# Five first slices of w1 issued from two queues, and one warm-up matmul fewer, in a SiLU MLP with its gradients

## The chip, the core and the metric

The kernel runs on one core of one Trainium2 chip. The metric is the device time of one execution in microseconds, as the median of several executions. The compute engines are TensorE (PE; its weight loads are listed apart as PEld), VectorE (DVE), ScalarE (ACT) and GpSimd (POOL). SyncE (SP) here only issues DMA transfers. ScalarE can issue them too, from a queue of its own. "SPq" and "ACTq" in the profile are the issuing of transfers by these two engines.

## The reference

```python
B, S, D, F = 1, 2048, 640, 1536          # all bf16
def _fwd_reference(x, w1, w2):
    h = jnp.einsum("bsd,df->bsf", x, w1)
    h = jax.nn.silu(h)
    out = jnp.einsum("bsf,fd->bsd", h, w2)
    return out

def reference(x, w1, w2, grad_out):
    _out, _vjp = jax.vjp(_fwd_reference, x, w1, w2)
    return (_out, *_vjp(grad_out))       # out, grad x, grad w1, grad w2
```

It is a two-layer perceptron with SiLU between the layers, forward and backward.

## The kernel before

The 2048 rows are worked in four chunks `c` of 512 (`SC`). For a chunk, TensorE computes h (line 204: `w1` slices times the transposed x), ScalarE makes a = silu(h) (line 213) and, with VectorE, the factor of the derivative (lines 217 to 220). TensorE then computes the gradient of a (line 254, finished by VectorE on line 261) and, in `sd_phase` (line 270), the chunk's out and its grad x. The transposed a, grad h, out and grad x go through DRAM scratch tensors (`aT_scr`, `ghT_scr`, `oT_scr`, `gxT_scr`) and come back transposed by DMA. After the four chunks two long stages make grad w2 (line 359) and grad w1 (lines 389 and 408). A matmul here has 128 x 128 weights and, nearly always, 512 columns.

The order of the instructions on each engine is that of the program as the tile framework schedules it, and each DMA issued takes one of eight completion semaphores in turn ("lanes"). A DMA that reuses a lane waits for the transfer that had it before.

What matters here is the head of the program, lines 143 to 210:

- Before the kernel's body the engines meet at an entry wait. `start_before_entry_wait` (line 16) takes the instructions of a given list, with what stands ahead of them on the same engine, and puts them in front of that engine's entry wait. The list is called `early`.
- VectorE fills a tile `warm` (line 144). TensorE runs `NWARM` = 21 matmuls of 128 columns on it (line 148), whose results nobody reads.
- SP issues the load of the first 128 rows of x (`x_nat`, q = 0) and ScalarE that of the next 128 (q = 1), line 171.
- SP then loads the first 1024 columns (`GC`) of w1 in slices of 128 rows: slices 0, 1 and 2 by one DMA each, ahead of the entry wait, and slices 3 and 4 together by one DMA after it (lines 177 and 178). A slice is 128 x 1024 bf16, 256 KB.
- Behind them on SP follow a DMA transpose that fills the second half of the first chunk's xT (line 179), the other 512 columns of w1 (line 180), w2 (line 183), the first chunk of grad_out transposed (line 184) and the transposed weights (lines 186 and 187).
- ScalarE, after its one load, loads its table and runs a small SiLU (line 182).
- `pe_x` (line 189): TensorE transposes the two loaded blocks of x in ten matmuls (line 195) into three PSUM tiles, and VectorE, ScalarE and VectorE copy these to the first half (`HC` = 256 columns) of xT (line 200). The first copy holds the rows of D that slice 0 of w1 meets, the second those of slices 1 and 2, the third those of slices 3 and 4.
- `h_first` (line 230): for slice after slice of w1, eight matmuls (ft 0 to 7) of 256 columns on that first half (line 235). So slice k is first needed by the matmul of number 8k, counted from 0. The eight sums need all eight PSUM banks: ft 6 takes the bank that ScalarE's copy empties. After the 40 matmuls of this kind come those on the second half of xT (line 237).

Of the kernel before, what the change touches and what calls it, by code (L numbers as in the profile page):

```python
# [15 lines left out]
def start_before_entry_wait(nc, names):  # L16

    def move(nc):
        blocks = nc.m.functions[0].blocks
        entry, home = blocks[0].instructions, blocks[1].instructions
        for engine in {i.engine for i in home if i.name in names}:
            mine = [i for i in home if i.engine == engine]
            last = max(k for k, i in enumerate(mine) if i.name in names)
            moved = mine[: last + 1]
            gate = next(
                k
                for k, i in enumerate(entry)  # L30
                if i.engine == engine and isinstance(i, mybir.InstEventSemaphore)
            )
            taken = {i.name for i in moved}
            for k in reversed(range(len(home))):
                if home[k].name in taken:
                    del home[k]
            for i in reversed(moved):
                entry.insert(gate, i)

    nc.at_finalize(move)  # L40
# [22 lines left out]
def kernel(  # L63
# [11 lines left out]
    nc = tc.nc  # L75
# [8 lines left out]
    F = w1.shape[1]  # L84
    ST, DT, FT = S // P, D // P, F // P
# [4 lines left out]
    NFC = F // FC  # L90
    FB = FC // P
    LAG = 2
    NWARM = 21
    HC = 2 * P
    NG = 8
    NCOPY = FT - NG
    GC = NG * P
# [16 lines left out]
    w1_v = w1.rearrange("(dt p) f -> p dt f", p=P)  # L114
# [19 lines left out]
    with ExitStack() as mctx:  # L134
# [9 lines left out]
        early = [nc.vector.memset(warm[:], 1.0)]  # L144
        warm_a = cpool.tile([P, 1], FP32, name="warm_a")
        wp = ps_h.tile([P, SC], FP32, name="wp", tag="hp")
        for i in range(NWARM):
            early.append(nc.tensor.matmul(wp[:, 0:P], lhsT=warm[:], rhs=warm[:], start=True, stop=True))  # L148
# [4 lines left out]
        w1_nat = w1pool.tile([P, DT, F], dt_in, name="w1_nat", tag="w1a")  # L153
# [16 lines left out]
        def load_x(eng, q):  # L170
            return eng.dma_start(out=x_nat[:, q, :], in_=x_v[:, q, :])

        def load_w1(lo, hi, cols):
            return nc.sync.dma_start(out=w1_nat[:, lo:hi, cols], in_=w1_v[:, lo:hi, cols])

        early += [load_x(nc.sync, 0), load_x(nc.scalar, 1)]
        early += [load_w1(k, k + 1, slice(0, GC)) for k in range(3)]
        load_w1(3, DT, slice(0, GC))
        nc.sync.dma_start_transpose(out=xT_next[:, :, HC:SC], in_=x2[HC:SC, :])
        load_w1(0, DT, slice(GC, F))  # L180
        start_before_entry_wait(nc, {i.ins.name for i in early})
        nc.scalar.activation(warm_a[:], warm[:, 0:1], ACT.Silu)
        nc.sync.dma_start(out=w2_nat[:], in_=w2_v[:])
# [101 lines left out]
        for c in range(NCH):  # L285
# [15 lines left out]
            if c == 0:  # L301
                h_first(xT, aT, ghT)
                nc.sync.dma_start(
                    out=aT_scr[:, c * SC:(c + 1) * SC].rearrange("(ft p) s -> p ft s", p=P), in_=aT[:]
                )
                sd_phase(c, w2_nat, aT, oT_scr)
                for ft in range(FT):
                    g_group(ft, goT, ghT)
                nc.sync.dma_start(
                    out=ghT_scr[:, c * SC:(c + 1) * SC].rearrange("(ft p) s -> p ft s", p=P), in_=ghT[:]  # L310
# [4 lines left out]
            for i in range(FT + LAG):  # L315
# [7 lines left out]
                out=aT_scr[:, c * SC:(c + 1) * SC].rearrange("(ft p) s -> p ft s", p=P), in_=aT[:]  # L323
            )
            nc.sync.dma_start(
                out=ghT_scr[:, c * SC:(c + 1) * SC].rearrange("(ft p) s -> p ft s", p=P), in_=ghT[:]
# [7 lines left out]
    with ExitStack() as fctx:  # L334
# [17 lines left out]
        k = 0  # L352
# [26 lines left out]
        k = 0  # L379
        for fc in range(NFC):  # L380
            gh_blk = gh_blks[fc]
            for dt_ in range(DT):
                if dt_ == DT // 2:
                    store_gw2(fc)
                if fc == NFC - 1 and dt_ == DT - 1:
                    for k, (lo, hi) in enumerate(((0, FC - P), (FC - P, FC))):
# [12 lines left out]
                        else:  # L399
                            nc.vector.tensor_copy(out=g1[:, lo:hi], in_=gp[:, lo:hi])  # L400
                        last_store = nc.sync.dma_start(
                            out=gw1_v[:, dt_, fc * FC + lo:fc * FC + hi], in_=g1[:, lo:hi]
# [49 lines left out]
```

## Time and profile before

| What | Value |
|---|---|
| median of 5 runs | 320.8 us (320.39, 320.17, 320.8, 321.26, 320.91) |
| the profiled execution | 320.42 us, of which the profile's span is 318.6 us |
| TensorE busy | 314.0 us of the span |
| VectorE, ScalarE, GpSimd busy | 103.1, 77.2 and 0.7 us |
| DMA | 67.02 MB, mean 210 GB/s |

Times within the profile are counted from the start of its span, in microseconds. A timeline merges instructions of one kind that follow each other: it gives the start, the time from the first start to the last end, the engine, the line, the operation, what it writes and reads, and the count. In brackets stands the idle time before it and what ended that. The time of a DMA issue is that of the issuing engine; the transfer itself lands later, which the list of DMA issues tells as microseconds from issue to landing.

### The profile page before, as it was taken

What the parts mean: (1) busy time and instruction counts of PE and PEld (TensorE: products, weight loads), DVE (VectorE), ACT (ScalarE), POOL (GpSimd) and SP (SyncE); (2) the same over time, 40 slices, a digit from 0 to 9 for tenths busy, and PEclk for the clock granted to TensorE, in tenths of its full rate; (3) what the DMA queues carried; (4) which work ended last, traced back from release to release, by engine and by line L of the source; (5) the groups of instructions that cost most, each with busy time, mean ns of one, the idle gap of its engine ahead of it and who ended that gap; (6) DMA issues with size and microseconds to landing.
All of it is one profiled execution on the core that took longest, in us unless ns stands there. A gap on an engine that the chain in (4) does not pass through costs nothing.

```text
span 318.6 us, 3597 instructions
## 1 busy us (share of the span) xinstructions
PE 314.0 (99%) x1499; PEld 149.3 (47%) x1527; DVE 103.1 (32%) x182; ACT 77.2 (24%) x139; POOL 0.7 (0%) x6
## 2 busy tenths in 40 slices
PE   9999999999999999999999999999999999999996
PEld 8744444444444444444444444444444444444443
DVE  1594641477410187700147741000000100001001
ACT  2781000644201354311064420111100001001100
POOL 0000000000000000000000000000000000000000
PEclk9999999999999999999999999999999999999999
DMA  9989999999899866382534089919999999997211
GB/s 245 347 170 213 236 264 246 347 288 309 249 238 320 211 207 165 105 290 84 165 115 134 0 273 263 208 30 294 248 240 255 241 216 347 220 264 218 67 39 45
DMA packets 147729, 67.02 MB, mean 210 GB/s; under 512 B 113921, under 2 KB 147073, under 8 KB 147713
## 3 DMA queue, kind: packets, MB, share of 16 engines
q1 hardware_dynamic: 147568, 66.62, 82.6%
q8 instruction: 12, 0.20, 0.2%
q10 hardware_dynamic: 144, 0.16, 0.1%
q14 instruction: 5, 0.03, 0.0%
HBM read 9.18 MB, written 28.97 MB: 120 GB/s over the span
## 4 chain that ended last, share of the span: by engine, by line
PE 99%; issue 1%; DVE 0%; DVEq 0%
PE hp L270 32%; PE hp L204 16%; PE hp L254 16%; PE hp L359 16%; PE hp L408 15%; PE hp L389 1%; PE wp L148 1%; PE tp L195 0%; DVE g L400 0%; DVE warm L144 0%; DVEq L400 0%; DVEq L436 0%
## 5 line engine op out<-in xcount | busy, mean ns | idle before, releaser
L204 PE MATMUL hp<-xT,w_nat 128*128 128x512 bf16 (+1 forms) x272 | 57.5, 352 | 0.4
L254 PE MATMUL hp<-goT,w2T 128*128 128x512 bf16 x238 | 56.8, 379 | 0.1
L270 PE MATMUL hp<-aT,w_nat 128*128 128x512 bf16 x235 | 52.2, 379 | 0.3
L270 PE MATMUL hp<-ghT,w1T 128*128 128x512 bf16 x236 | 52.2, 379 | 0.2
L359 PE MATMUL hp<-a_blk,go_nat 128*128 128x512 bf16 x235 | 51.7, 379 | 0.3
L408 PE MATMUL hp<-gh_blk,x_nat 128*128 128x512 bf16 x220 | 48.3, 379 | 0.2
L278 ACT ACTIVATE oT<-hp 128x512 bf16<-128x512 f32 x24 | 14.3, 598 | 106.5 <-PE hp L270 106.5
L204 PEld LDWEIGHTS <-w_nat 128*128 128x128 bf16 x280 | 27.8, 100 | 25.0 <-DMA w_nat<-in_w_dram 0.2
L213 ACT ACTIVATE aT<-hp 128x512 bf16<-128x512 f32 x48 | 28.6, 606 | 36.0 <-PE hp L204 36.0
L270 PEld LDWEIGHTS <-w1T 128*128 128x128 bf16 x240 | 23.5, 98 | 28.3
L254 PEld LDWEIGHTS <-w2T 128*128 128x128 bf16 x240 | 23.5, 98 | 28.3
L359 PEld LDWEIGHTS <-go_nat 128*128 128x128 bf16 x240 | 23.5, 98 | 28.3
L270 PEld LDWEIGHTS <-w_nat 128*128 128x128 bf16 x240 | 23.4, 98 | 28.4
L261 DVE SCALAR_TENSOR_TENSOR ghT<-ghT,hp 128x512 bf16<-128x512 bf16 x48 | 32.5, 682 | 7.3 <-PE hp L254 7.3
L280 DVE CAST oT<-hp 128x512 bf16<-128x512 f32 x16 | 11.1, 692 | 72.4 <-PE hp L270 72.4
L408 PEld LDWEIGHTS <-x_nat 128*128 128x128 bf16 x224 | 21.9, 98 | 26.4
L220 DVE SCALAR_TENSOR_TENSOR ghT<-aT,v 128x512 bf16<-128x512 bf16 x48 | 32.6, 687 | 0.3
L219 DVE TENSOR_SCALAR v<-t 128x512 bf16<-128x512 f32 x48 | 20.2, 426 | 27.7 <-ACT t L217 27.7
L217 ACT ACTIVATE t<-hp 128x512 f32<-128x512 f32 x44 | 26.1, 598 | 0.5 <-DVE v L219 0.5
L419 DVE CAST g<-hp 128x512 bf16<-128x512 f32 x7 | 4.8, 692 | 47.0 <-PE hp L408 26.6
L369 DVE CAST g2T<-hp 128x512 bf16<-128x512 f32 x7 | 4.8, 692 | 46.1 <-PE hp L359 46.1
L367 ACT ACTIVATE g2T<-hp 128x512 bf16<-128x512 f32 x8 | 4.8, 597 | 47.0 <-PE hp L359 47.0
(22 smaller groups left out, 27.1 us busy)
## 6 DMA issues: line engine op xcount, KB each, us to landing
aT_scr<-aT SPq DMA_DIRECT2D x4, 1536.0 KB, 6.3
ghT_scr<-ghT SPq DMA_DIRECT2D x4, 1536.0 KB, 8.1
out_dram<-o_sb SPq DMA_DIRECT2D x8, 640.0 KB, 3.4
oT_scr<-oT SPq DMA_DIRECT2D x4, 640.0 KB, 4.3
go_nat<-in_grad_out_dram SPq DMA_DIRECT2D x4, 640.0 KB, 6.5
gxT_scr<-oT SPq DMA_DIRECT2D x4, 640.0 KB, 5.0
w_nat<-in_w_dram SPq DMA_DIRECT2D x1, 1920.0 KB, 12.8
x_nat<-in_x_dram SPq DMA_DIRECT2D x3, 640.0 KB, 7.2
```

Of the source, the lines that this page charges most:

```text
L204: nc.tensor.matmul(hp[:, cols], lhsT=w1_nat[:, dt_, ft * P:(ft + 1) * P], rhs=xT[:, dt_, cols], start=(dt_ == 0), stop=(dt_ == DT - 1),)
L213: nc.scalar.activation(aT[:, ft, :], hp[:], ACT.Silu)
L217: nc.scalar.activation(t[:], hp[:], ACT.Tanh, scale=0.5)
L219: nc.vector.tensor_scalar(out=v[:], in0=t[:], scalar1=-0.5, scalar2=0.5, op0=ALU.mult, op1=ALU.add)
L220: nc.vector.scalar_tensor_tensor(out=ghT[:, ft, :], in0=aT[:, ft, :], scalar=1.0, in1=v[:], op0=ALU.subtract, op1=ALU.mult)
L254: nc.tensor.matmul(gp[:], lhsT=w2T[:, dt_, ft * P:(ft + 1) * P], rhs=goT[:, dt_, :], start=(dt_ == 0), stop=(dt_ == DT - 1),)
L261: nc.vector.scalar_tensor_tensor(out=ghT[:, ft, :], in0=ghT[:, ft, :], scalar=1.0, in1=gp[:], op0=ALU.add, op1=ALU.mult)
L270: nc.tensor.matmul(op_[:], lhsT=w_all[:, ft, dt_ * P:(dt_ + 1) * P], rhs=rhs_all[:, ft, :], start=(ft == 0), stop=(ft == FT - 1),)
L278: nc.scalar.activation(oT[:, dt_, :], op_[:], ACT.Copy)
L280: nc.vector.tensor_copy(out=oT[:, dt_, :], in_=op_[:])
L359: nc.tensor.matmul(gp[:], lhsT=go_nat[:, st, dt_ * P:(dt_ + 1) * P], rhs=a_blk[:, st, :], start=(st == 0), stop=(st == ST - 1),)
L408: nc.tensor.matmul(gp[:], lhsT=x_nat[:, st, dt_ * P:(dt_ + 1) * P], rhs=gh_blk[:, st, :], start=(st == 0), stop=(st == ST - 1),)
```

## The change

The five slices of w1 become five DMAs. Slices 0, 2 and 3 are issued by SP and slices 1 and 4 by ScalarE, all ahead of the entry waits. One warm-up matmul is dropped.

```diff
-    NWARM = 21
+    NWARM = 20
...
-        def load_w1(lo, hi, cols):
-            return nc.sync.dma_start(out=w1_nat[:, lo:hi, cols], in_=w1_v[:, lo:hi, cols])
+        def load_w1(eng, lo, hi, cols):
+            return eng.dma_start(out=w1_nat[:, lo:hi, cols], in_=w1_v[:, lo:hi, cols])
 
         early += [load_x(nc.sync, 0), load_x(nc.scalar, 1)]
-        early += [load_w1(k, k + 1, slice(0, GC)) for k in range(3)]
-        load_w1(3, DT, slice(0, GC))
+        for k, eng in enumerate((nc.sync, nc.scalar, nc.sync, nc.sync, nc.scalar)):
+            early.append(load_w1(eng, k, k + 1, slice(0, GC)))
         nc.sync.dma_start_transpose(out=xT_next[:, :, HC:SC], in_=x2[HC:SC, :])
-        load_w1(0, DT, slice(GC, F))
+        load_w1(nc.sync, 0, DT, slice(GC, F))
         start_before_entry_wait(nc, {i.ins.name for i in early})
```

In the built program SP has one instruction fewer and ScalarE has two DMA issues more, ahead of its entry wait and its table load. SP still has four DMAs ahead of its own entry wait. The lanes of all later transfers move on by one, and so do their waits. In two places SP's order changes: the transpose of x for chunk 2 (line 160) stands ahead of the store of chunk 0's out (line 281) instead of behind it, and the transpose of grad_out for chunk 2 (line 165) ahead of the store of chunk 0's grad h (line 309).

## The prediction

> **What bounds the kernel now.** I read the page first (span, busy times, chain), then the timeline of the first 22 us, then the head again by weight loads, by half-microsecond windows and by DMA issues.
>
> ```profile
> span 318.6 us, 3597 instructions
> ...
> PE 314.0 (99%) x1499; PEld 149.3 (47%) x1527; DVE 103.1 (32%) x182; ACT 77.2 (24%) x139; POOL 0.7 (0%) x6
> ...
> PE 99%; issue 1%; DVE 0%; DVEq 0%
> ```
>
> TensorE is the bound from end to end. All that a change of the loads can touch is TensorE's idle or slow time in the head, so the head is read instruction by instruction (timeline; start, length, engine, line, count):
>
> ```profile
> 0.09 0.40 SPq L171 DMA_DIRECT2D x_nat<-in_x_dram  x1
> 0.21 0.38 ACTq L171 DMA_DIRECT2D x_nat<-in_x_dram  x1
> ...
> 0.50 2.42 PE L148 MATMUL wp<-warm 128*128 128x128 bf16 x21 [0.50 <-DVE warm L144]
> 0.54 1.89 SPq L174 DMA_DIRECT2D w_nat<-in_w_dram  x4
> ...
> 0.74 1.28 ACT L182 ACT_TABLE_LOAD   x1 [0.74 <-DVEq L436]
> ...
> 2.47 1.49 SPq L179 DMA_TRANSPOSE xT<-in_x_dram  x1
> ...
> 2.72 1.27 PE L195 MATMUL tp<-ident,x_nat 128*128 128x128 bf16 x10
> 3.60 0.85 DVE L200 COPY xT<-tp 128x256 bf16<-128x256 bf16 x2 [3.16 <-PE tp L195]
> ...
> 3.81 0.59 ACT L200 COPY xT<-tp 128x512 bf16<-128x512 bf16 x1 [1.58 <-PE tp L195]
> ...
> 7.51 10.11 PEld L204 LDWEIGHTS <-w_nat 128*128 128x128 bf16 x76 [0.20 <-DMA w_nat<-in_w_dram]
> ```
>
> TensorE starts at 0.50 and from then on waits for data in one listed place: 0.20 us before the weight load at 7.51, the first use of slice 3. That is 0.20 us of the loader. A load normally follows the last by 0.109 us here (next view), so the matmul row loses about 0.20 - 0.11 = 0.09 us. The first matmul on h starts at 3.94, just after the first copy of xT ends (a copy of 0.29 us from 3.60, so 3.89). The weight loads, one for each matmul, tell TensorE's pace:
>
> ```profile
> 4.11 1.65 PEld L204 LDWEIGHTS <-w_nat 128*128 128x128 bf16 x8
> 5.80 1.52 PEld L204 LDWEIGHTS <-w_nat 128*128 128x128 bf16 x14
> ```
>
> Eight loads from 4.11 to 5.80 are (5.80 - 4.11) / 8 = 0.211 us each; from 5.80 on it is (1.52 - 0.10) / 13 = 0.109. So TensorE runs at half pace until 5.80, though the profile's granted clock reads 1.00 in every row. A microsecond lost or won before 5.80 is worth half a microsecond of work. The DMA side, by windows (TensorE, weight loads, VectorE, ScalarE, GpSimd, clock, DMA share, GB/s) and by issues (time from issue to landing last):
>
> ```profile
> 2.00:2.50 0.50, 0.50 (x7) 0.50 (x6) 0.00 (x0) 0.22 (x2) 0.00 (x0) 1.00 1.07 373
> 2.50:3.00 0.50, 0.50 (x7) 0.47 (x6) 0.00 (x0) 0.00 (x0) 0.00 (x0) 1.00 1.06 408
> ```
>
> ```profile
> w_nat<-in_w_dram SPq DMA_DIRECT2D x3, 256.0 KB, 3.7
> ...
> w_nat<-in_w_dram SPq DMA_DIRECT2D x1, 512.0 KB, 5.4
> ...
> x_nat<-in_x_dram SPq DMA_DIRECT2D x1, 160.0 KB, 2.6
> x_nat<-in_x_dram ACTq DMA_DIRECT2D x1, 160.0 KB, 2.8
> ```
>
> ```profile
> w_nat<-in_w_dram SPq DMA_DIRECT2D x1, 256.0 KB, 3.2
> ```
>
> The last line is slice 0 alone: 0.54 + 3.2 = 3.74. The five copies of line 174 land after 3.2, 3.7, 4.6, 5.4 and 6.6 us: slice 1 at about 1.0 + 3.7 = 4.7, slice 2 at 1.47 + 4.6 = 6.1, slices 3 and 4 at 2.04 + 5.4 = 7.4. The DMA engines are full from 2.0 on. Slices 3 and 4 are late because of the bytes ahead of them, not because of when they are issued.
>
> **The change part by part.**
>
> *One warm-up matmul fewer.* Its pace is (2.72 - 0.50) / 21 = 0.106 us. The first transpose would be free to start at 2.61, but x lands at 0.09 + 2.6 = 2.69, so it gains 0.03 us of wall time, at half pace 0.015. Bounds: 0, and 0.106 / 2 = 0.05 if x lands earlier. I take 0.015, by the landing row.
>
> *Slices 3 and 4 issued ahead of the entry wait.* SP issues its fourth slice at about 1.47 instead of 2.04, ScalarE slice 4 earlier still. With the engines full (1.07, 1.06) the same 320 KB of x and 1280 KB of w1 must pass before the fifth slice is in. If the engines take the two queues in turn, the order is x, x, slice 0 (SP), 1 (ACT), 2 (SP), 4 (ACT), 3 (SP): the one that is needed first of the last two comes last. So slice 3 lands where the pair landed. Bounds: 0, and all of the 0.09 us if slice 3 comes ahead of 4. I take 0, by the two full windows.
>
> *Slice 0 now has a rival for the engines.* Slice 1, from ScalarE at about 0.65, can run beside slice 0 from SP at 0.54. The two x blocks show how two queues share: issued 0.12 apart they landed at 2.69 and 0.21 + 2.8 = 3.01, one after the other and not both at the end. That speaks for slice 0 keeping its 3.74; it may come as late as 3.89, when the xT copy ends, at no cost. Bounds: 0, and slice 1 wholly ahead, 256 KB at 373 GB/s = 0.70 us, landing 4.44: 4.44 - 3.91 = 0.53 us of wait, half of that 0.26. I take 0.
>
> The Trainium skill speaks against the change, in "DMA: Bandwidth & Descriptors", section "Issuing engines are not separate DMA queues": transfers from several engines run on the same 16 DMA engines and interleave, and several issuers save only the issuing time. By it the sum below stays; by a reading of two queues as twice the bandwidth slice 3 would be 0.09 us to the good.
>
> *What is queued behind ScalarE's two new issues.* At SP's spacing (0.54 + 1.89 for four, so 0.47 each) they delay ScalarE's table load from 0.74 to about 1.7; it ends at 3.0 and the small SiLU (0.2 us) at 3.2. The next work of ScalarE is its xT copy at 3.81, released by TensorE: 0.6 us of cover, cost 0. Were the cover gone, the copy's result is wanted only by slice 1, eight matmuls after 3.94 (about 5.6), and its bank by ft 6 at 3.94 + 6 x 0.211 = 5.2; it ends at 4.40 now. Another 0.8 us is free, then it costs half of each microsecond.
>
> *What moves on SP.* One DMA less after the entry wait: the xT transpose, the rest of w1, w2 and grad_out are issued some 0.4 us earlier, into engines that are full. The rest of w1 now waits for the lane of the second x block (3.01, before SP gets there at 3.6), w2 for the first x block's, grad_out for slice 1's (4.7, wanted at about 6.5). Cost 0.
>
> *The two swaps in the middle of SP's order.*
>
> ```profile
> 43.65 0.59 SPq L281 DMA_DIRECT2D oT_scr<-oT  x1
> 44.33 8.45 SPq L160 DMA_TRANSPOSE xT<-in_x_dram  x1
> ```
>
> The store goes behind an issue of 8.45 us, and the read-back of it, next but one on SP, waits for its landing (8.0 us in the list of the oT issues) some 5 us longer. The store's buffer is written again at 85.5 by ScalarE, over 25 us later; the grad h store slips in the same way from 63.2, by the 7.25 us of its transpose and these 5 us, and its buffer is next written in chunk 2, after 108. Cost 0.
>
> Sum against the profiled execution: 318.6 - 0.015 + 0 + 0 + 0 = 318.6 of span, and the 1.8 us that lie outside it (320.42 - 318.6) stay. That execution is 0.4 us under the median of 320.8. The forecast is thus the median itself, 320.8, with 320.8 - 0.05 - 0.09 = 320.7 and 320.8 + 0.26 = 321.1 as bounds of the known terms. The five runs spread over 1.09 us; I give the forecast 320.4 to 321.4.
>
> **The rivals.**
>
> *Slice 0 comes late and TensorE speeds up later (slower).* Place: the first load of line 204, at 3.77. The wait costs 0.26 at most by itself. But if the full pace is granted for activity, a hole before 5.80 may put it off. It came 5.80 - 0.50 = 5.3 us after the first matmul; put off by d it costs d / 2, between 0 and 2.65 us, and I take the middle, 1.3. Then 320.8 + 0.2 + 1.3 = 322.3. It decides from a landing of slice 0 after about 3.9. For it: slice 0 has only 0.15 us of slack. Against it: the order of the x blocks, and a hole that the head already has between transposes and h (ten transposes at 0.106 from 2.72 end at 3.78, so 3.94 - 3.78 = 0.16 us).
>
> The Trainium skill, "TensorE: Matmul & The Clock Gate", Part 1, holds that the full clock comes after a busy window of 3.4 us that runs free of the kernel. By it one missed window costs 3.4 / 2 = 1.7 us, an estimate, and this rival would give 322.7.
>
> *TensorE speeds up earlier (faster).* The same dependence, with x and the slices a little earlier and the waits gone. Known gains end at 0.05 + 0.09 = 0.14, too little to be told. Only an earlier pace change can do more: at best at 3.94, (5.80 - 3.94) / 2 = 0.93, so 319.9. Nothing in the head gets denser except by 0.03 us, so mostly the spread of the runs speaks for it.
>
> *The third slice's wait does go.* Slice 3 ahead of 4: 320.8 - 0.09 - 0.015 = 320.7, within no change.
>
> **How the numbers follow.** What a measurement of this kernel can tell from no change is about 0.2%, 0.64 us. Forecast with the last rival: 0.48. Late slice 0 or a later pace: 0.32, as it has the larger price. Earlier pace, or a median that falls on the low side: 0.20. The predicted time is 320.8. The range runs from 320.0, most of the way to 319.9, up to 322.0, within the slower case.
>
> **What would show it.** The wait before slice 3 near 7.4 still there and on a DMA: the shared engines are right. Slice 0 landing after 3.9 and a wait before the first load of line 204: the slower rival. The pace of the weight loads changing far from 5.8: the pace decides, in either direction. A wait of ScalarE's copy at 3.81 for its table, or any TensorE wait after 8 us, would make my cover wrong.

## The result, and the profile after

The changed kernel took 320.99 us (median of 27 runs, 320.38 to 323.62) against 320.61 us for the kernel before in the same comparison (46 runs, 320.17 to 321.26). The ratio is 1.0021 with a 95% interval of 1.0011 to 1.003: slower by about 0.2%. It agrees with the averages of the runs, 321.30 and 320.64 us; the medians differ by 0.38 us, or 0.12%. The fastest runs of the two kernels lie 0.2 us apart, but ten of the 27 runs took 321.4 us or more, and the kernel before has none there. The loss is in the upper part of the spread, so a typical run loses less than a bad one.

The profiled execution of the changed kernel is one of these: 321.77 us with a span of 320.0, so again 1.8 us lie outside. The page, in its span, busy times and chain:

```profile
span 320.0 us, 3597 instructions
...
PE 314.0 (98%) x1498; PEld 149.0 (47%) x1526; DVE 103.0 (32%) x182; ACT 77.2 (24%) x139; POOL 0.7 (0%) x6
...
PE 96%; DMA 2%; issue 1%; ACTq 0%; DVE 0%; DVEq 0%
```

TensorE is as busy as before, 314.0 us. What is new is a DMA share in the chain. The head, in the timeline (columns as before):

```profile
0.54 1.36 SPq L174 DMA_DIRECT2D w_nat<-in_w_dram  x3
0.62 0.94 ACTq L174 DMA_DIRECT2D w_nat<-in_w_dram  x2
...
1.67 1.28 ACT L182 ACT_TABLE_LOAD   x1 [1.67 <-ACTq L436]
2.04 2.19 SPq L179 DMA_TRANSPOSE xT<-in_x_dram  x1
2.83 0.98 PEld L195 LDWEIGHTS <-x_nat 128*128 128x128 bf16 x10 [0.27 <-DMA x_nat<-in_x_dram]
...
3.90 0.59 ACT L200 COPY xT<-tp 128x512 bf16<-128x512 bf16 x1 [0.73 <-PE tp L195]
...
4.41 1.40 PEld L204 LDWEIGHTS <-w_nat 128*128 128x128 bf16 x8 [0.60 <-DMA w_nat<-in_w_dram]
4.41 1.68 PE L204 MATMUL hp<-xT,w_nat 128*128 128x256 bf16 x8 [0.34 <-DMA w_nat<-in_w_dram]
...
7.11 1.97 PEld L204 LDWEIGHTS <-w_nat 128*128 128x128 bf16 x19 [1.30 <-DMA w_nat<-in_w_dram]
7.12 2.14 PE L204 MATMUL hp<-xT,w_nat 128*128 128x256 bf16 x18 [1.02 <-DMA w_nat<-in_w_dram]
```

Two waits stand where there was none: before the first load on slice 0 (at 4.41) and, after exactly eight loads, before the first load on slice 1 (at 7.11). The wait before slice 3, near 7.5 in the kernel before, is gone; slice 3 is wanted only near 8.8 now. In the kernel before, the loads of line 204 up to that wait form one row:

```profile
3.77 3.54 PEld L204 LDWEIGHTS <-w_nat 128*128 128x128 bf16 x24
```

These are all the waits of TensorE and its loader on a DMA in the changed kernel, over the whole span (engine, line, what was waited for; us in total, times, longest):

```profile
PEld L204 <- DMA w_nat<-in_w_dram: 1.9, 2, 1.3
PE hp L204 <- DMA w_nat<-in_w_dram: 1.4, 2, 1.0
PEld L195 <- DMA x_nat<-in_x_dram: 0.3, 1, 0.3
```

The last is the wait for x ahead of the transposes (x was in at 2.79, before at 2.64). It is over well before slice 0 is in.

The difference of the two spans, 320.0 - 318.6 = 1.4 us, is accounted for as follows. The pace changes from half to full at about 5.8 in both profiles. By then the kernel before has begun ten weight loads of line 204 and the changed one eight; two at 0.109 us make 0.22. The loads on slice 1 start 1.30 us after the last one ended, and the profile before loses 0.11 there by its normal spacing: 1.19. The 0.09 before slice 3 is won. Together 0.22 + 1.19 - 0.09 = 1.32 of 1.4.

Why the two slices are late is told by the issues, each in a window of its own: engine, size, us from issue to landing. The first is slice 0, the second slice 1:

```profile
w_nat<-in_w_dram SPq DMA_DIRECT2D x1, 256.0 KB, 3.8
```

```profile
w_nat<-in_w_dram ACTq DMA_DIRECT2D x1, 256.0 KB, 6.5
```

Slice 1 was issued at 0.62, earlier than before, and landed at 7.1; before, it landed at 4.7. The DMA queues between 3 and 4 us show its new path (queue: packets, MB, share of 16 engines; q1 holds what SP issues, q10 what ScalarE issues). First the kernel before, then the changed one:

```profile
q1 hardware_dynamic: 184, 0.33, 112.0%
```

```profile
q10 hardware_dynamic: 107, 0.20, 61.1%
q1 hardware_dynamic: 64, 0.10, 34.6%
```

Before, all 0.33 MB of that microsecond came through SP's queue. After, two thirds came through ScalarE's. These bytes are slice 1's, and by themselves no loss: slice 1 is the second to be needed. A slice is spread over 16 DMA engines, and TensorE goes on only when the last of them has reported: the loads start at 4.41 and 7.11, 0.04 us after the last reports of slices 0 and 1, at 4.37 and 7.07. The trace's semaphore records give that report for each engine; here are the landing times of each slice, as the median of the 16 engines, the 13th and the last (us):

```
             slice 0            slice 1            slice 2            slice 3            slice 4
before       3.53 3.59 3.73     4.18 4.36 4.74     5.12 5.95 6.08     7.43 7.45 7.47 (3 and 4 together)
changed      3.51 3.61 4.37     4.31 4.83 7.07     5.29 5.58 7.27     8.38 8.56 8.61     5.92 8.33 8.37
```

The typical engine kept nearly the old order and the old times for slices 0 to 2. Most engines worked off one transfer after the other: between 3.2 and 3.8 us the records count 77 packets of q10, slice 1's, and only 15 of q1. A few engines fell behind, and these decide. The 2 KB packets from 6.56 to 7.2 us form three chains, each with a packet every 0.08 us, and in each chain q10 and q1 alternate strictly: an engine with work left in both queues serves them by turns here.

The chain that closes slice 1 last can be followed back by the packets' times (the records don't name the engine). Slice 1's first packet started at 4.07 and took 1.47 us instead of 0.08. Its other seven started from 5.62 to 6.58, 0.16 us apart, with slice 2's eight packets between them. So the engine lost 1.39 us to one long packet and, by an estimate from these numbers, 8 x 0.08 = 0.64 us to the turns with slice 2. In one queue, slice 2 would have stood behind slice 1. By this estimate the turns are about half of the 1.19 us; the long packet is the rest. The transpose of x, which SP issued 0.43 us earlier than before, has no part in it: its first packets started at 5.75 (5.81 before), after the long one.

### The profile page after: what moved, and what is told of

Same layout as the page of the kernel before. It is cut to its first block, busy times and chain, and to the rows that moved or that the text cites. A ratio compares the mean times of both kernels' runs of the same rounds, so it can differ in the third digit from the quotient of the medians.

```text
span 320.0 us, 3597 instructions
## 1 busy us (share of the span) xinstructions
PE 314.0 (98%) x1498; PEld 149.0 (47%) x1526; DVE 103.0 (32%) x182; ACT 77.2 (24%) x139; POOL 0.7 (0%) x6
## 4 chain that ended last, share of the span: by engine, by line
PE 96%; DMA 2%; issue 1%; ACTq 0%; DVE 0%; DVEq 0%
PE hp L270 32%; PE hp L254 16%; PE hp L359 16%; PE hp L204 16%; PE hp L408 15%; DMA w_nat<-in_w_dram 2%; PE hp L389 1%; ACTq L171 0%; DVE g L400 0%; DVEq L400 0%; ACTq L436 0%
```

## The experiments

All ratios are to the kernel before on the same chip, with their 95% intervals. The edits are to the changed kernel unless something else is said. The first group shares one chip (kernel before: 320.36 us), the second another (321.13), the third a third (320.64).

**All five slices on SP.** If the second queue is the cause, the loss goes though one warm-up matmul is still missing and the slices are still ahead of the entry wait.

```diff
-        for k, eng in enumerate((nc.sync, nc.scalar, nc.sync, nc.sync, nc.scalar)):
+        for k, eng in enumerate((nc.sync,) * DT):
```

> The changed kernel with all five slices on SP's queue, still one DMA each, ahead of the entry wait and with 20 warm-up matmuls. Theory A (two queues share each DMA engine, so slices that are needed early lose turns to later ones on the slowest engines): the loss of 0.21% goes, ratio to before 0.9995 to 1.0005, slice 1 lands before 5.3 us in full and TensorE waits less than 0.3 us before the fifth slice. Theory B (the dropped warm-up matmul, or the issue ahead of the entry wait, costs the time): ratio stays at 1.001 to 1.003. Theory C (the two swaps in the middle of SP's order): here that order is as before, so the loss goes as with A, but waits in the head stay.

Measured: 320.15 us (12 runs), ratio 1.0001 (0.9988 to 1.0015). The timeline of its weight loads:

```profile
3.81 6.22 PEld L204 LDWEIGHTS <-w_nat 128*128 128x128 bf16 x57
```

There is no wait before any slice. They were in at 3.76, 4.49, 5.42, 6.05 and 6.74, each in order, and slice 3 more than a microsecond before its time in the kernel before. A new wait of 0.48 us for w2 appears near 17 us (line 270), where TensorE arrives earlier. SP's order in the middle of the program is that of the kernel before in this kernel, so by itself it doesn't part the second queue from the two swaps. The profile after does, with no TensorE wait on a DMA behind the head, and a run below has a swap without the loss.

**The kernel before with 20 warm-ups.** This is the dropped matmul alone.

```diff
-    NWARM = 21
+    NWARM = 20
```

> The kernel before with 20 warm-up matmuls instead of 21, nothing else. Theory A: no change, ratio 0.9995 to 1.0003. Theory B: slower, 1.001 to 1.003, with an idle TensorE between the last warm-up matmul and the first transpose.

Measured: 320.51 us (11 runs), ratio 1.0005 (0.9997 to 1.0014). The interval is narrow and ends below the middle of the change's own. The old wait stays, and nothing else appears:

```profile
3.68 3.35 PEld L204 LDWEIGHTS <-w_nat 128*128 128x128 bf16 x24
7.43 2.62 PEld L204 LDWEIGHTS <-w_nat 128*128 128x128 bf16 x25 [0.40 <-DMA w_nat<-in_w_dram]
```

**The changed kernel with 21 warm-ups.** The same question from the other side.

```diff
-    NWARM = 20
+    NWARM = 21
```

> The changed kernel with 21 warm-up matmuls, the slices still alternating. Theory A: as the changed kernel, ratio 1.001 to 1.003. Theory B: the loss goes, 0.9995 to 1.0005. Theory C: as A.

Measured: 320.81 us (12 runs), ratio 1.0018 (1.0004 to 1.0033). The loss and both waits are there with the old warm-up (on this chip the intervals of this kernel and of the one-queue kernel overlap; the averages, 320.94 and 320.37, lie 0.57 us apart):

```profile
4.26 1.41 PEld L204 LDWEIGHTS <-w_nat 128*128 128x128 bf16 x8 [0.53 <-DMA w_nat<-in_w_dram]
6.10 3.94 PEld L204 LDWEIGHTS <-w_nat 128*128 128x128 bf16 x36 [0.42 <-DMA w_nat<-in_w_dram]
```

The warm-up has no share that could be measured.

**Slices 0 to 2 on SP, 3 and 4 on ScalarE.** If the two queues kept the order of need, this would be the best split: the slices needed last are in the second queue. If they take turns, slices 3 and 4 take turns from 0 and 1.

```diff
-        for k, eng in enumerate((nc.sync, nc.scalar, nc.sync, nc.sync, nc.scalar)):
+        for k, eng in enumerate((nc.sync, nc.sync, nc.sync, nc.scalar, nc.scalar)):
```

> The changed kernel with slices 0, 1 and 2 on SP's queue and 3 and 4 on ScalarE's, 20 warm-up matmuls; the number of lanes and SP's order are those of the changed kernel. Theory A in the form that any traffic on the second queue takes turns from the early slices: slower, ratio 1.001 to 1.003, slices 0 to 2 land later than before (over 4.0, 5.0 and 6.3 us in full). In the form that only a slice which stands on ScalarE's own queue comes late: slices 0 to 2 land as before (3.7, 4.7, 6.1) and the ratio is within 0.9995 to 1.0005. Theory C: 1.002 as the changed kernel, with no wait in the head.

Measured: 323.36 us (6 runs), ratio 1.0089 (1.0055 to 1.0122): four times the loss, and far above the 1.001 to 1.003 that was expected. Timeline of the weight loads:

```profile
5.02 0.77 PEld L204 LDWEIGHTS <-w_nat 128*128 128x128 bf16 x8 [1.44 <-DMA w_nat<-in_w_dram]
6.99 3.12 PEld L204 LDWEIGHTS <-w_nat 128*128 128x128 bf16 x16 [1.20 <-DMA w_nat<-in_w_dram]
```

Slice 3, wanted fourth, was in on its last engine at 6.14, and slice 1, wanted second, at 6.95. On the median engine too slice 3 (4.18) came ahead of slice 1 (5.35): it was issued at 0.62, slice 1 at 0.99. The order on that engine is the order of issue over both queues. Transfers taken from the two queues by turns would give the same order, and no run here tells these two apart, since the two issuers alternate in time in all of them. The loss was also larger than the waits, and the windows say why (window, its length, TensorE's busy time and instructions, granted clock, DMA share, GB/s):

```profile
5.00:6.70 1.70, 1.05 (x8) 1.00 1.05 305
6.80:8.40 1.60, 1.41 (x7) 0.50 1.17 213
8.40:10.10 1.70, 1.70 (x10) 0.50 1.10 320
10.30:12.00 1.70, 1.70 (x18) 1.00 1.07 356
```

The full clock had been granted at 3.37. It was taken back at 6.78 and given again at 10.19, 3.41 us later. In the 3.41 us before it was taken back, TensorE had been idle for about 2 (1.44 busy, from 3.37 to 6.78).

**Only slice 4 on ScalarE.** The same competition with half the bytes.

```diff
-        for k, eng in enumerate((nc.sync, nc.scalar, nc.sync, nc.sync, nc.scalar)):
+        for k, eng in enumerate((nc.sync, nc.sync, nc.sync, nc.sync, nc.scalar)):
```

> The changed kernel with slices 0 to 3 on SP's queue and slice 4 alone on ScalarE's, 20 warm-up matmuls. Theory A (the DMA engines serve the two queues by turns, so 256 KB that are needed last are moved ahead of slices that are needed first): between one queue (1.0001) and two late slices on ScalarE's queue (1.0089), ratio 1.001 to 1.005, and one of slices 0 to 2 lands in full later than before by 0.3 us or more. Rival D (only slice 0's delay matters, or the loss needs both issues): as one queue, 0.999 to 1.001.

Measured: 320.56 us (12 runs), ratio 0.9993 (0.998 to 1.0007). It is not slower than the kernel before, so the number that the two-queue theory gave was missed, and the rival's, 0.999 to 1.001, was met. Slice 0 was late (4.17 on the last engine) and had a wait, the others had none:

```profile
4.21 5.79 PEld L204 LDWEIGHTS <-w_nat 128*128 128x128 bf16 x46 [0.41 <-DMA w_nat<-in_w_dram]
```

Slice 4 was in on the median engine at 4.25, ahead of slices 1, 2 and 3. Against the one-queue kernel on this chip (320.27) the median is 0.3 us higher, but the intervals overlap, so a cost of one slice on ScalarE's queue isn't shown. This kernel also has the store of chunk 0's out behind the transpose of x, as the changed kernel has, and no loss by it.

**Both x blocks and all slices on SP.** If any second queue costs, moving x's second block to SP should gain a little.

```diff
-        early += [load_x(nc.sync, 0), load_x(nc.scalar, 1)]
-        for k, eng in enumerate((nc.sync, nc.scalar, nc.sync, nc.sync, nc.scalar)):
+        early += [load_x(nc.sync, 0), load_x(nc.sync, 1)]
+        for k, eng in enumerate((nc.sync,) * DT):
```

> The one-queue kernel with the second block of x on SP too, so that ScalarE issues no load: one queue for the whole head. Theory A: the order of the issues is then the order of the bytes; the block of x is issued 0.3 us later and each slice about 0.45 us later, which costs nothing as long as the engines are full, ratio 0.9985 to 1.001. Rival E (a second issuer saves time, and x on ScalarE's queue is worth its place): slower by 0.3 us or more, 1.001 or above, by a wait for x or slice 0.

Measured: 320.96 us (12 runs), ratio 1.0006 (0.9991 to 1.0021): inconclusive against the kernel before. It is 0.7 us slower than the one-queue kernel with x on two queues (320.27; the intervals, 0.9991 to 1.0021 and 0.9969 to 0.999, don't meet), so the gain didn't come, and the rival that x on ScalarE's queue is worth its place is the better supported. With x issued first on one queue, slice 0 is issued at 1.00 instead of 0.54. The profile has a long wait for slice 0:

```profile
5.38 1.64 PEld L204 LDWEIGHTS <-w_nat 128*128 128x128 bf16 x16 [1.76 <-DMA w_nat<-in_w_dram]
```

Slice 0 was in at 3.71 on the median engine, 3.83 on the 13th and 5.34 on the last. So a lagging engine occurs with one queue too. The second queue isn't its only source: a packet that started at 2.74 took 1.76 us here.

**Slices 3 and 4 on ScalarE, behind its small SiLU.** The idea was to have the second queue's bytes start only after slice 0.

```diff
-        for k, eng in enumerate((nc.sync, nc.scalar, nc.sync, nc.sync, nc.scalar)):
-            early.append(load_w1(eng, k, k + 1, slice(0, GC)))
+        for k in range(3):
+            early.append(load_w1(nc.sync, k, k + 1, slice(0, GC)))
...
         nc.scalar.activation(warm_a[:], warm[:, 0:1], ACT.Silu)
+        for k in range(3, DT):
+            load_w1(nc.scalar, k, k + 1, slice(0, GC))
```

> Slices 0, 1 and 2 on SP ahead of the entry wait, 3 and 4 on ScalarE's queue behind its table load and small SiLU, so issued near 2.3 and 2.7 us instead of 0.6 and 1.1; 20 warm-up matmuls. Theory A: ScalarE's packets reach the engines after slice 0 has gone and beside slices 1 and 2, so slice 0 lands as before (3.8 at most in full) and the loss is clearly below the 1.0089 of the early issue: 1.000 to 1.004. Rival F (any use of ScalarE's queue for these slices costs, whenever issued): as the early issue, 1.006 or more.

Measured: 321.66 us (12 runs), ratio 1.0028 (1.0009 to 1.0046). The delay didn't come about: the trace has the two issues at 0.80 and 1.17, beside the table load, not behind it. It is a milder form of the kernel with slices 3 and 4 on ScalarE. Slice 0 was on time (3.66), slice 1 was in on the last engine at 6.51:

```profile
3.70 1.55 PEld L206 LDWEIGHTS <-w_nat 128*128 128x128 bf16 x8
6.55 0.77 PEld L206 LDWEIGHTS <-w_nat 128*128 128x128 bf16 x8 [1.30 <-DMA w_nat<-in_w_dram]
7.90 10.99 PEld L206 LDWEIGHTS <-w_nat 128*128 128x128 bf16 x84 [0.58 <-DMA w_nat<-in_w_dram]
```

The third row's wait is for slice 2, in at 7.86 on the last engine (6.08 in the kernel before). As in the other kernel, slice 3 was issued (0.80) ahead of slice 1 (0.99) and came ahead of it on the median engine. The ratio agrees with a cost of the second queue, but as the bytes weren't held back it can't tell what a delay would do.

**The one-queue kernel again**, on this second chip; the edit is that of the first experiment.

> The one-queue kernel of the first group once more, all five slices as one DMA each on SP ahead of the entry wait, 20 warm-up matmuls, for a second profile and more runs. Theory A: 0.9990 to 1.0005, no wait before any of the five slices. If the wait before slice 3 that the kernel before has (0.09 us) is the whole gain, the ratio is 0.9997.

Measured: 320.27 us (12 runs, 319.37 to 320.95), ratio 0.9979 (0.9969 to 0.999). Here it is faster than the kernel before, by more than was expected; on the first chip the interval held 1. This profile has a wait of 0.18 us for slice 1, whose last engine reported at 5.22, where none was expected. By the medians it is both times faster than every kernel with a second queue for slices that it shared a chip with (320.15 against 320.81 and 323.36; 320.27 against 320.56 and 321.66); clear of noise are the differences to the two kernels with slices 3 and 4 on ScalarE (323.36 and 321.66).

**Both x blocks on ScalarE, all slices on SP.** Two queues, for other data: x is needed first and would now share the engines with slice 0 and slice 1.

```diff
-        early += [load_x(nc.sync, 0), load_x(nc.scalar, 1)]
-        for k, eng in enumerate((nc.sync, nc.scalar, nc.sync, nc.sync, nc.scalar)):
+        early += [load_x(nc.scalar, 0), load_x(nc.scalar, 1)]
+        for k, eng in enumerate((nc.sync,) * DT):
```

> One queue for the five slices (SP, all ahead of the entry wait), and both blocks of x on ScalarE's queue, so that the transfer needed first of all shares the engines with slices that are needed later. Theory A: the second block of x takes turns with slices and lands after 3.2 us in full (3.0 to 3.2 in the kernels that issue the first block from SP), the transposes start or pause later, ratio 1.0005 to 1.005. Rival G (two queues are harmless where the bytes are few, and slice 0 gains by being issued at 0.1): 0.997 to 1.000.

Measured: 322.03 us (6 runs, 321.72 to 322.78), ratio 1.0044 (1.0029 to 1.0058).

```profile
3.42 0.45 PEld L195 LDWEIGHTS <-x_nat 128*128 128x128 bf16 x5 [0.87 <-DMA x_nat<-in_x_dram]
4.50 0.45 PEld L195 LDWEIGHTS <-x_nat 128*128 128x128 bf16 x5 [0.62 <-DMA x_nat<-in_x_dram]
```

On the median engine the order was slice 0 (2.64), x block 0 (3.08), slice 1 (3.84), x block 1 (4.30). That is turns between the queues, transfer by transfer, but it is the order of issue as well (0.08, 0.21, 0.54 and 0.62), and x block 1 was issued 0.41 us later than before, behind slice 1. No slice was waited for, and all six runs lie above the highest of the kernel before (321.43). So the loss needs no lagging engine here: data needed first landed behind data that was issued ahead of it in the other queue. It doesn't show that the queues take turns.

**One queue, and w2 in two DMAs.** The one-queue kernel had a wait for w2 near 17 us; this takes it away.

```diff
-        for k, eng in enumerate((nc.sync, nc.scalar, nc.sync, nc.sync, nc.scalar)):
+        for k, eng in enumerate((nc.sync,) * DT):
...
-        nc.sync.dma_start(out=w2_nat[:], in_=w2_v[:])
+        for k in (0, FT // 2):
+            nc.sync.dma_start(out=w2_nat[:, k:k + FT // 2, :], in_=w2_v[:, k:k + FT // 2, :])
```

> The one-queue kernel with the load of w2 as two DMAs of 960 KB. Theory A says nothing of it; it is a trial of what bounds next: the one-queue kernel waits for w2 near 17 us in both of its profiles (0.3 and 0.5 us of the weight loader). With halves that wait should go: ratio 0.0003 to 0.001 below the one-queue kernel's, 0.997 to 0.9995.

Measured: 320.38 us (12 runs), ratio 0.9997 (0.9983 to 1.001). The wait is gone from the profile, and no gain can be measured. A wait of 0.37 us for slice 0 and one run of 322.64 us came instead. Its second use is as a one-queue kernel beside the next one.

**The changed kernel again**, unedited, beside the next one.

> The changed kernel itself, beside the one-queue kernels on one chip and for a second profile. Theory A: 1.001 to 1.003, with a wait of TensorE before slice 0 or slice 1 and the last DMA engine's share of slice 0 or 1 landing 0.4 us or more after that of the other engines.

Measured: 321.42 us (12 runs), ratio 1.0026 (1.0011 to 1.0042), its profiled execution 322.39 us. On this one chip the interval lies wholly above that of the one-queue kernel with w2 in two DMAs (0.9983 to 1.001); the medians are 1.0 us apart. This profile shows another form of the same loss. The loads from 5.2 to 8.4 us, and those after 8.7 (two windows of the timeline):

```profile
5.12 3.33 PEld L204 LDWEIGHTS <-w_nat 128*128 128x128 bf16 x17 [1.50 <-DMA w_nat<-in_w_dram]
```

```profile
8.71 1.41 PEld L204 LDWEIGHTS <-w_nat 128*128 128x128 bf16 x13
```

Only slice 0 was waited for (5.08 on its last engine, 3.57 on the median), but the full pace came at about 8.6: 17 loads in 3.33 us, some 0.2 each, where the 13 later ones take 1.41, some 0.11 each.

**The kernel before, with slices 3 and 4 as two DMAs behind the entry wait.** This is the one useful part of the change without its second queue. The edit is to the kernel before.

```diff
-        load_w1(3, DT, slice(0, GC))
+        for k in range(3, DT):
+            load_w1(k, k + 1, slice(0, GC))
```

> The kernel before with slices 3 and 4 as two DMAs, still behind SP's entry wait, 21 warm-up matmuls, all on SP. If the one-queue kernel gains because slice 3 has a semaphore of its own: the same gain, 0.9975 to 0.9995, slice 3 in full before 7.0 us and no wait before it. If it gains by the issue ahead of the entry wait: no change, 0.9995 to 1.0005, with the wait before slice 3 still there.

Measured: 320.31 us (12 runs, 319.8 to 320.7), ratio 0.9985 (0.9976 to 0.9994): faster than the kernel before, and 1.1 us faster than the changed kernel on the same chip (321.42).

```profile
3.68 6.41 PEld L205 LDWEIGHTS <-w_nat 128*128 128x128 bf16 x46
```

Slice 3 was in at 6.42 and slice 4 at 7.10; there is no wait. Slice 3 need not be issued earlier. Its own completion is enough, as in the pair TensorE waits for slice 4 too. The wait that goes is worth only some 0.1 us of the 0.33 between the medians; the rest isn't explained.

## Why the prediction was right or wrong

The time lies in the range, but the forecast of no change was wrong: 0.21% is just past the 0.2% that the prediction named as its bound, and the interval leaves no change out. That 320.99 us came so near the forecast 320.8 is luck: the forecast took the median of five runs for the kernel before, 320.8, and over 46 runs it is 320.61.

**The step that failed is "Slice 0 now has a rival for the engines".** It was taken at nothing, with 0.26 us as its upper bound. The reason given was that the two x blocks on two queues landed one after the other. That holds for the typical engine, and says nothing of the slowest. The step read a landing as one moment, at which a certain number of bytes has passed. It is that of the slowest of 16 engines: slice 0 was in on 13 engines at 3.61, even earlier than the forecast 3.74, and on the last at 4.37. The late slice 0 cost 0.22 us, inside the bound. What broke the bound was never priced: slice 1. It had a slack of 0.9 us (landing 4.7, wanted at about 5.6), as the forecast's own rows show, and it stood in the queue that was said to run beside slice 0. In the profile it came at 7.07, at full pace, and cost 1.19 us, about half of it by the turns with slice 2 and the rest by one long packet. That execution is one of the slower ones; over all runs the loss is 0.38 us by the medians and 0.66 us by the averages.

**Rivals.** The slower rival had the right place and only half of the mechanism: slice 0 late, with the price in the change of pace. In the profile after, the pace changed when it did before, and the price was the wait for slice 1. In the second profile of the changed kernel the rival did happen as told: slice 0 at 5.08, the pace at 8.6, 322.39 us against its 322.3. The medians, 320.99 and 321.42, lie lower. The faster rival didn't come. "The third slice's wait does go" came true for a reason that wasn't meant: TensorE is later.

**Slices 3 and 4.** Right that issuing slice 3 earlier brings nothing with the engines full, and wrong that it lands where the pair did: it landed at 8.61 against 7.47, which cost nothing only because TensorE was late as well. The forecast put the order x, x, 0, 1, 2, 4, 3, and the median engine kept it. It held the bytes ahead to be the reason why slice 3 is late, and missed that the wait goes with one queue and the old moment of issue: with a DMA of its own, issued at 2.04 as the pair was, slice 3 was in at 6.42.

**What held.** One warm-up matmul fewer: nothing that can be measured, from both sides. ScalarE's two issues: its table load began at 1.67 (1.7 was forecast), its SiLU ended at 3.17 (3.2), and its xT copy waited for TensorE. SP's moved issues and the two swaps: no wait of TensorE on them, though only the transpose of x went out earlier (2.04, before 2.47). Its issue took 2.19 us instead of 1.49, so the rest of w1 followed at 4.28, later than before (4.01). The sign that the forecast named, "Slice 0 landing after 3.9 and a wait before the first load of line 204: the slower rival", came, and pointed to the right side; it says nothing of slice 1, where most of the time went in the profile.

**The rule.** The Trainium skill, "DMA: Bandwidth & Descriptors", section "Issuing engines are not separate DMA queues", has it that transfers from several engines share the 16 DMA engines and interleave, so that only issuing time is saved. The queue rows agree (0.20 and 0.10 MB side by side between 3 and 4 us). The forecast read it as "no gain"; these runs show that with data needed in an order, interleaving can be a loss.

**What stays open:** why single DMA engines lag, and why by so much in some runs. The second queue doesn't seem to make them lag. Of the five slices' 640 packets, 17 took over 0.3 us in the kernel before and 10 and 9 in the two profiles of the changed one; 8, 10 and 20 in the two one-queue profiles and the one with x on SP too. The longest was 1.47 us in the changed kernel (0.69 before), but 1.34 and 1.76 with one queue (the second one-queue profile and the one with x on SP too). What two queues add is that on an engine that is behind, a slice needed later takes every second packet. That was followed on one engine of one profile; how much of the average loss it makes isn't shown.

## What to carry to other kernels

When the DMA engines are full and the data is wanted in a known order, issue it in that order over all queues, and give each piece that is waited for its own completion. Of pieces that follow closely, one queue was the safer here for the slices of w1, since on an engine that is behind, the second queue takes turns from the piece that is wanted next. It is no rule for everything: the two blocks of x did better on two queues. Price every piece that follows in such a change by the slowest of the engines, and compare that with the moment at which it is wanted: the second piece can cost more than the first.

## What the runs showed that was not expected

- The change from half to full pace moves by several microseconds between executions: it lay between 3.37 and about 8.6 us in the 14 profiles of this study, 5.8 in that of the kernel before. At half pace in between, each microsecond is worth half a microsecond, so the two profiles of the changed kernel (5.8 and 8.6) differ by some 1.4 us from this alone, an estimate. The granted clock reads 1.00 from the start in all 14 and doesn't show it; the spacing of the weight loads does. The trace's clock records begin only at the change (5.77 in the kernel before, 5.75 in the changed one; its second profile has none).
- The second half-pace stretch, after a hole, lasted 3.41 us (6.78 to 10.19, the kernel with slices 3 and 4 on ScalarE), and about 2 us of idle time in 3.41 stood ahead of it, while the changed kernel kept its full pace with 1.03 us idle in one such stretch (2.38 busy of 3.41, in the window from 5.75 to 9.16). The Trainium skill, "TensorE: Matmul & The Clock Gate", Part 1, holds that the clock is judged in windows of 3.4 us that run free of the kernel; the length agrees.
- Two DMA issues that stand behind an activation in ScalarE's program (the kernel with slices 3 and 4 behind the small SiLU) went out at 0.80 and 1.17, beside the table load.
